# Seven-quarter W2 products, running sums added by an accumulating DMA, and a fixed weave in an attention and mixture-of-experts kernel

## The chip, the cores and the metric

The kernel runs on one core of a Trainium2 chip. The metric is device microseconds of one execution; lower is better. The kernel before took 844.76 us (median of 4 runs, 843.47 to 848.35); one profiled execution of it, from which the readings below come, had a span of 838.8 us (840.54 us as it was timed, a little less than any of the four). The names in profiles: PE is TensorE (PEld its weight loads), ACT is ScalarE, DVE is VectorE, POOL is GpSimd, SP is SyncE. An engine's name with a q is its DMA issuing or its sequencer.

## The reference, cut to what matters

```python
N, D, E, F = (3072, 512, 8, 1024)          # tokens, model width, experts, hidden width

def reference(q, k, v, proj, w_gate, w1, w2):
    x = masked_attention(q, k, v, proj)    # 4 batches of 768 tokens, 8 heads; [cut]
    P = exp(x @ w_gate - max)              # then 8 rounds of row and column scaling; [cut]
    out = zeros((N, D))
    for e in range(E):
        h = maximum(x @ w1[e], 0.0)        # "W1 product"
        ye = h @ w2[e]                     # "W2 product"
        out += P[:, e:e + 1] * ye
    return out
```

Every expert works on every token, so the second half of the program is 8 experts x 4 batches of 768 tokens. The change touches experts 1 to 7: 28 batches, which I name by expert and by b = 0 to 3. Expert 0 runs in the shadow of attention and routing.

## The kernel before: the parts that matter

The W1 product (`hidden`) already uses a Strassen-Winograd scheme: it is cut into 2 x 2 quarters and made of seven quarter products instead of eight, at the price of a few additions. GpSimd makes the sums of the weights (`quarters_of_w`), VectorE those of x. The W2 product (`combine`) is plain, and VectorE adds its result, times the routing weight, to the running sums `acc`. The W2 product of one batch is woven into the W1 product of the next, so that each engine's waits are covered by the other product. In the code, `pin(...)` keeps an instruction at its place in the program's order, and PSUM is the memory that matmuls write to.

```python
def load_w(e, which, pin=False):                     # 1 MB, cast to fp16 by GpSimd's DMA
    ...
    ins = nc.gpsimd.dma_start(out=t, in_=src)

def quarters_of_w(e):                                # called at b == 2 of the expert before
    if (e, 1) not in weights:
        load_w(e, 1, pin=True)
    ...
    s = spool.tile([P, 3, 2, F // 2], F16, tag="s1")
    pin(nc.gpsimd.tensor_tensor(s[:, 0], a21, a22, op=Alu.add))
    pin(nc.gpsimd.tensor_tensor(a21, a11, a21, op=Alu.subtract))
    pin(nc.gpsimd.tensor_tensor(s[:, 1], s[:, 0], a11, op=Alu.subtract))
    pin(nc.gpsimd.tensor_tensor(s[:, 2], a12, s[:, 1], op=Alu.subtract))

def combine(e, b):                                   # plain W2 product
    for j in range(J):                               # 6 blocks of 128 tokens
        yp = ... # a PSUM bank, 128 x 512
        for fo in range(FO):                         # 8 matmuls of 512 columns
            yield nc.tensor.matmul(yp, hT[:, fo, j * P:(j + 1) * P], w2[:, fo, :], ...)
            if fo == FO - 1:
                nc.vector.scalar_tensor_tensor(out=acc[:, blk, :], in0=yp, scalar=pw_[-1][:, blk, e:e + 1],
                                               in1=acc[:, blk, :], op0=Alu.mult, op1=Alu.add)
                if e == E - 1:
                    nc.sync.dma_start(out=outv[b, j], in_=acc[:, blk, :])
    # [cut: expert 0, the scaling in expert 1, the yields]

def woven(n):                                        # one step of each product in turn
    h = hidden(*work[n]) ...
    c = combine(*work[n - 1]) ...
    while more:
        more = run(h, True);  yield 650
        more = run(c, True) or more;  yield 650
```

The view of the output is `outv = out.rearrange("(b r j m) d -> b j m r d", ...)`: one block's output has the shape 4 x 32 x 512, which will matter.

The softmax here doesn't subtract the row's maximum and nothing guards it: scores larger than these inputs give would overflow.

## Time and profile before

| | before |
|---|---|
| median time | 844.76 us |
| span of the profiled run | 838.8 us |
| busy share of TensorE, VectorE, ScalarE, GpSimd | 94%, 52%, 47%, 20% |
| period of a batch (last ReLU copy of one batch to that of the next, on ScalarE) | 19.9 us in 25 of 27, 21.61 us in two of expert 1 |
| last matmul to the end of the span | 13.0 us |

These are lines of the page of the kernel before. The first line under part 1 is busy time and share of each engine. PEclk is TensorE's granted clock in tenths of full speed in 40 slices of the span. The line after it is the chain of waits that ended last, by engine. A group's line gives busy time, mean ns of one and idle time before it. The last line is a DMA issue with its size and the median us from issue to landing.

```profile
span 838.8 us, 13662 instructions
...
PE 786.6 (94%) x5404; PEld 427.1 (51%) x5404; DVE 440.2 (52%) x789; ACT 394.9 (47%) x698; POOL 165.8 (20%) x196
...
PEclk9879999999999999999999999999999999999997
...
PE 83%; DVE 6%; DMA 5%; ACT 2%; SPq 1%; issue 1%; POOL 1%; ACTq 0%; POOLq 0%; DVEq 0%
...
L155 PE MATMUL yp<-t,hT 128*128 128x512 f16 x1440 | 385.1, 379 | 0.0
...
L161 DVE SCALAR_TENSOR_TENSOR acc<-yp,p,acc 128x512 f32<-128x512 f32 x168 | 125.9, 749 | 114.0 <-PE yp L155 111.6
...
t<-in_moe_w_dram POOLq DMA_DIRECT2D x16, 1024.0 KB, 8.8
```

TensorE bounds the kernel: 83% of the chain are its matmuls. One batch period seen as a stretch says the same; the columns are the stretch, its length, busy us of PE, PEld, DVE, ACT and POOL with instruction counts, the clock, the DMA share and GB/s.

```profile
455.07:474.97 19.90, 19.76 (x106) 10.16 (x105) 10.73 (x19) 7.73 (x17) 0.00 (x0) 1.00 0.00 1
```

TensorE works 19.76 of 19.90 us at full clock, VectorE about half, GpSimd not at all. Once per expert GpSimd prepares the next W1. Its timeline (start, length, instruction, in brackets the idle time before it and what ended it) is:

```profile
417.05 0.75 POOL L120 DMA_DIRECT2D t<-in_moe_w_dram  x1 [58.10 <-PE d L520]
425.00 2.12 POOL L136 TENSOR_TENSOR s<-t 128x1024 f16<-128x1024 f16 x1 [7.20 <-DMA t<-in_moe_w_dram]
```

It issues the load, waits 7.20 us for it, and then runs four additions of 2.12 us. In this part of the program its queue holds nothing else but the load of W2.

### The profile page before, as it was taken

What the parts mean: (1) busy time and instruction counts of PE and PEld (TensorE: products, weight loads), DVE (VectorE), ACT (ScalarE), POOL (GpSimd) and SP (SyncE); (2) the same over time, 40 slices, a digit from 0 to 9 for tenths busy, and PEclk for the clock granted to TensorE, in tenths of its full rate; (3) what the DMA queues carried; (4) which work ended last, traced back from release to release, by engine and by line L of the source; (5) the groups of instructions that cost most, each with busy time, mean ns of one, the idle gap of its engine ahead of it and who ended that gap; (6) DMA issues with size and microseconds to landing.
All of it is one profiled execution on the core that took longest, in us unless ns stands there. A gap on an engine that the chain in (4) does not pass through costs nothing.

```text
span 838.8 us, 13662 instructions
## 1 busy us (share of the span) xinstructions
PE 786.6 (94%) x5404; PEld 427.1 (51%) x5404; DVE 440.2 (52%) x789; ACT 394.9 (47%) x698; POOL 165.8 (20%) x196
## 2 busy tenths in 40 slices
PE   3869999999889999999999999999999999999993
PEld 1546656666544544555555555555555555555551
DVE  3434646654476555555555555555555555555551
ACT  0857767678634555533333333333333333333330
POOL 7645245534031000400040004001300310000000
PEclk9879999999999999999999999999999999999997
DMA  6966677531020300230032023002300230001222
GB/s 176 263 155 155 136 182 192 130 73 27 1 51 2 51 0 1 51 51 1 3 51 48 1 47 47 9 1 51 50 1 1 51 51 1 1 0 52 77 81 92
DMA packets 31927, 50.60 MB, mean 60 GB/s; under 512 B 8504, under 2 KB 21304, under 8 KB 31864
## 3 DMA queue, kind: packets, MB, share of 16 engines
q0 software_dynamic: 16880, 33.30, 19.2%
q1 hardware_dynamic: 14316, 15.95, 7.0%
q8 instruction: 42, 0.69, 0.3%
q10 hardware_dynamic: 668, 0.49, 0.2%
q14 instruction: 21, 0.17, 0.1%
HBM read 53.14 MB, written 7.08 MB: 72 GB/s over the span
## 4 chain that ended last, share of the span: by engine, by line
PE 83%; DVE 6%; DMA 5%; ACT 2%; SPq 1%; issue 1%; POOL 1%; ACTq 0%; POOLq 0%; DVEq 0%
PE yp L155 34%; PE a L520 17%; PE d L520 14%; PE st L320 6%; PE hp L378 4%; DVE hT L529 4%; PE num L336 3%; PE yp L388 2%; ACT pt L323 2%; PE hp L177 1%; DMA ks<-t 1%; PE pr L243 1%; DMA v<-in_v_dram 1%; DMA acc<-in_q_dram 1%; DMA ds<-kb 1%
## 5 line engine op out<-in xcount | busy, mean ns | idle before, releaser
L155 PE MATMUL yp<-t,hT 128*128 128x512 f16 x1440 | 385.1, 379 | 0.0
L525 ACT COPY u<-a 128x384 f32<-128x384 f32 x336 | 161.1, 480 | 252.8 <-PE a L520 243.7
L529 DVE CUSTOM_DVE_ANT_0 hT<-d,u 128x384 f16<-128x384 f32 x336 | 179.3, 554 | 146.5 <-PE d L520 87.6
L155 PEld LDWEIGHTS <-hT 128*128 128x128 f16 x1440 | 140.9, 98 | 121.8 <-issue 0.8
L161 DVE SCALAR_TENSOR_TENSOR acc<-yp,p,acc 128x512 f32<-128x512 f32 x168 | 125.9, 749 | 114.0 <-PE yp L155 111.6
L323 ACT ACTIVATE pt<-st 128x768 f16<-128x768 f32 x192 | 147.2, 809 | 71.7 <-PE st L320 71.0
L520 PEld LDWEIGHTS <-t 128*128 128x128 f16 x896 | 87.8, 98 | 78.7 <-issue 10.8
L320 PE MATMUL st<-qs,ks 71*128 71x384 f16 x384 | 97.4, 336 | 18.4 <-DMA ks<-t 7.5
L520 PE MATMUL d<-xd,t 128*128 128x384 f16 x448 | 109.5, 326 | 3.9
L520 PEld LDWEIGHTS <-s 128*128 128x128 f16 x672 | 65.6, 98 | 87.0 <-issue 8.3
L520 PE MATMUL a<-xT,s 128*128 128x384 f16 x448 | 109.3, 326 | 0.0
L555 ACT ACTIVATE hT<-a 128x384 f16<-128x384 f32 x112 | 55.0, 491 | 73.9 <-PE a L520 73.4
L120 POOL DMA_DIRECT2D t<-in_moe_w_dram x16 | 13.5, 846 | 374.0 <-PE d L520 295.2
L336 PEld LDWEIGHTS <-pt 128*128 128x128 f16 x1152 | 62.3, 99 | 28.0 <-issue 3.0
L336 PE MATMUL num<-va,pt 128*128 128x65 f16 x1152 | 68.2, 196 | 0.6 <-ACT pt L323 0.6
L520 PE MATMUL a<-xd,s 128*128 128x384 f16 x224 | 55.1, 328 | 3.1 <-DVE xd L502 3.1
L520 PE MATMUL d<-xT,t 128*128 128x384 f16 x224 | 55.1, 328 | 0.0
L520 PE MATMUL a<-xT,t 128*128 128x384 f16 x224 | 55.0, 327 | 0.0
L320 PEld LDWEIGHTS <-ks 71*128 71x128 f16 x384 | 33.4, 100 | 39.3 <-issue 13.0
L232 POOL CAST t<-acc 128x768 f16<-128x768 f32 x32 | 26.3, 825 | 89.1 <-DVE acc L231 75.1
L381 DVE TENSOR_SCALAR hT<-hp 128x384 f16<-128x384 f32 x48 | 26.7, 555 | 28.6 <-PE hp L378 28.6
L378 PE MATMUL hp<-xT,t 128*128 128x384 f16 x192 | 39.0, 325 | 0.0
(74 smaller groups left out, 416.1 us busy)
## 6 DMA issues: line engine op xcount, KB each, us to landing
t<-in_moe_w_dram POOLq DMA_DIRECT2D x16, 1024.0 KB, 8.8
out_dram<-acc SPq DMA_DIRECT2D x24, 256.0 KB
acc<-in_k_dram POOLq DMA_DIRECT2D x7, 768.0 KB, 5.8
acc<-in_q_dram POOLq DMA_DIRECT2D x7, 768.0 KB, 5.9
v<-in_v_dram POOLq DMA_DIRECT2D x28, 192.0 KB, 4.6
ks<-t SPq DMA_DIRECT2D x64, 48.0 KB
qs<-t SPq DMA_DIRECT2D x56, 48.0 KB
acc<-in_k_dram SPq DMA_DIRECT2D x1, 768.0 KB
```

Of the source, the lines that this page charges most:

```text
L155: yield nc.tensor.matmul(yp, hT[:, fo, j * P:(j + 1) * P], w2[:, fo, :], start=(fo == 0), stop=(fo == FO - 1))
L161: nc.vector.scalar_tensor_tensor(out=acc[:, blk, :], in0=yp, scalar=pw_[-1][:, blk, e:e + 1], in1=acc[:, blk, :], op0=Alu.mult, op1=Alu.add)
L232: pin(nc.gpsimd.tensor_copy(t16s[name][:, c, :], trs[name][:, c, :]))
L320: pin(nc.tensor.matmul(st[:, i, 0:HT], d["k"][0:KR, h, kt * P:(kt + 1) * P], d["q"][0:KR, h, i * HT:(i + 1) * HT], start=True, stop=True))
L323: pin(nc.scalar.activation(out=pt, in_=st[:, :, 0:HT], func=Act.Exp, scale=scale))
L336: pin(nc.tensor.matmul(num[:, j * (D + 1):(j + 1) * (D + 1)], pf[:, j * P:(j + 1) * P], va[:, h, kt, :], start=(kt == 0 and j == 0), stop= ...
L378: pin(nc.tensor.matmul(hp[:, 0:HT], w1[:, do, fo * P:(fo + 1) * P], xT[:, do, b * S + t * HT:b * S + (t + 1) * HT], start=(do == 0), stop= ...
L381: pin(nc.vector.tensor_scalar(hT[:, fo, t * HT:(t + 1) * HT], hp[:, 0:HT], 0.0, None, op0=Alu.max))
L520: yield nc.tensor.matmul(bk, wq[wn][:, do, f * P:(f + 1) * P], xq[xn][:, do, :], start=first and do == 0, stop=do == 1, skip_group_check=True)
L525: nc.scalar.copy(t, bk)
L529: add(TENSOR_ADD_SAT, out=dst, in0=bk, in1=u, s0=3e38, s1=0.0)
L555: nc.scalar.activation(out=hT[:, f, hi], in_=a, func=Act.Relu)
```

## The change

The intent is to take TensorE's time down, since TensorE bounds the kernel. The W2 product is cut into quarters too: 3 pairs of token blocks x 7 products x 4 matmuls of 256 columns = 84 matmuls in place of 48 of 512. The additions this needs go where there was room. GpSimd makes the sums of W2 (`quarters_of_w2`, at b = 3), VectorE those of h (`sums_of_h`). Four of the seven results of a pair are read from one running PSUM bank by ScalarE, scaled, into a buffer `vt`, and one accumulating DMA in GpSimd's queue adds `vt` to `acc`. VectorE gathers the other three. The weave becomes a fixed string of steps: H is a step of the W1 product (`hidden`), C one of the W2 product (`mixed`).

```diff
+    def quarters_of_w2(e):                             # called at b == 3 of the expert before
         if (e, 2) not in weights:
+            load_w(e, 2, pin=True)
+        ...
+        pin(nc.gpsimd.tensor_tensor(t[:, 1], b22, b12, op=Alu.subtract))
+        pin(nc.gpsimd.tensor_tensor(b12, b12, b11, op=Alu.subtract))
+        pin(nc.gpsimd.tensor_tensor(t[:, 0], b22, b12, op=Alu.subtract))
+        pin(nc.gpsimd.tensor_tensor(t[:, 2], b21, t[:, 0], op=Alu.subtract))
+    def sums_of_h(e, b, i):                            # four VectorE operations, both operands in SBUF
+        pin(nc.vector.tensor_tensor(s_[:, 0], h21, h22, op=Alu.add))
+        pin(nc.vector.tensor_tensor(s_[:, 1], s_[:, 0], h11, op=Alu.subtract))
+        pin(nc.vector.tensor_tensor(h21, h11, h21, op=Alu.subtract))
+        pin(nc.vector.tensor_tensor(s_[:, 2], h12, s_[:, 1], op=Alu.subtract))
+    def mixed(e, b):
+        for i in range(J // 2):
+            vt = vkeep.tile([P, 4, DD // 2], F32, tag="v", name="vt")
+            ...                                        # 7 products; keep() for four, gather() for three
+            def keep(k, p):
+                pin(nc.scalar.activation(out=vt[:, k], in_=a, func=Act.Copy, scale=p))
+            def gather(k, src, p):
+                pin(nc.vector.scalar_tensor_tensor(out=dst, in0=src, scalar=p, in1=dst, ...))
+            for g, name in enumerate(ORDERS[i]):
+                step(name)
+                if g == 6:
+                    pin(nc.gpsimd.dma_start(out=acc[:, b, i], in_=vt, accum_op=Alu.add))
+                    if e == E - 1:                     # [cut: the last sum of all is done without it]
+                        pin((nc.gpsimd if final else nc.sync).dma_start(out=outv[b, j], in_=sums_of(b, j)...))
+    hspool = ctx.enter_context(tc.tile_pool(name="hspool", bufs=3))
+    vkeep = ctx.enter_context(tc.tile_pool(name="vkeep", bufs=3))
     def hidden(e, b):
         if b == 2 and e < E - 1:
             quarters_of_w(e + 1)
+        if b == 3 and e < E - 1:
+            quarters_of_w2(e + 1)
     def woven(n):
-        more = True
-        while more:
-            more = run(h, True); yield 650
-            more = run(c, True) or more; yield 650
+            plan = "HHCHCHCHCCH" + 3 * "HHCHCHCHCHCH" + "CH"
```

The cuts are the layout of `acc`, the pools that moved to make room, the sums of x, which are issued one at a time, and the pinned order of the W1 product and of expert 0.

## The prediction

> **What bounds it now.** In the view by stretches PE is busy 59.6 of each 60 us at clock 1.00; VectorE 32, ScalarE 23, GpSimd at most 10. The chain of waits from 380 us to the end is 92% matmuls (yp 48.7%, a 24.0%, d 19.4%). The timeline shows a 19.89 us period for each expert and batch (27 such periods): 56 matmuls of 384 columns at 162.5 ns (9.1 us), 48 of 512 at 216.7 ns (10.4 us), and two gaps of about 0.3 us.
>
> **What the change moves.** W2 products become 3 x 7 x 4 = 84 matmuls of 256 columns. The cost is linear (216.7/512 = 162.5/384), so 108.3 ns each: 9.1 us instead of 10.4. Weight loads keep up: attention's 65-column matmuls are 32 ns apart. A period is then 18.2 us, say 18.55 with gaps: 27 x 1.34 = 36 us off the critical path.
>
> Off the path, per period (estimated from like operations):
> - VectorE loses 6 x 749 ns, gains 12 fp16 additions of 512 (the 768-wide ones take 553 ns, so 0.42 us: 5.0 us) and 9 gathers of 256 (0.48 us: 4.3 us): 10.7 -> 16.0 us. 86% busy, in bursts of four additions (1.7 us).
> - ScalarE gains 12 scaled copies of 256 (about 0.38 us): 7.7 -> 12.3 us; expert 1's paired 0.72 us scalings cost about 3 us in all.
> - GpSimd gains three 512 KB accumulating DMAs per period and four more 2.12 us tensor operations per expert.
>
> **What gives some back.** GpSimd's order is load, four additions, then that period's accumulating DMAs, 12 times in all (W1 and W2 of six experts). Load and additions hold its queue 0.85 + 7.1 + 8.6 = 16.5 us, so the first sum's DMA leaves about 18 us into the period and lands 4 to 5 us later (768 KB loads land in 5.8). Its buffer (three, for three sums per period) is wanted again about 19.3 us in, and TensorE can run about a microsecond more: a 0 to 4 us stall. Second, VectorE's additions have two SBUF operands. The Trainium skill, "SBUF — State Buffer", section "Who interferes with whom", says these contend, as an exclusive lock, with a GpSimd instruction that reads SBUF. The trace agrees for another operation: the 192-wide kb scaling takes 0.39 to 0.77 us, ending when the GpSimd operation beside it ends. No run yet shows it for two-operand additions. If it holds in full, four additions behind four 2.1 us operations take 8 us, and y's single bank then stalls TensorE up to 5 us. Worst case 12 x 5 = 60 us; I take 1.4 us a time, 17 us.
>
> **Sum.** 844 - 36 + 3 + 17 = 828; leaning lower for gaps the fixed pattern removes: **826 us**, 80% range 806 to 868. Faster by over 2%: 0.52; within 2%: 0.28; slower: 0.20.
>
> **What would show it.** Right: period about 18.5 us for batches without weight preparation; 256-column matmuls 108 ns apart; in the two periods per expert with preparation, waits of ScalarE's vt copy on a DMA, and VectorE's hs additions lengthened from 0.42 towards 2 us beside GpSimd. Wrong: matmul spacing over 108 ns; waits spread over all periods (bursts on VectorE); vt waiting on DMAs everywhere (accumulating DMAs slower than 6 us each).
>
> **What would make it wrong.** Full lock on every addition (860 or more); or accumulating DMAs landing in 2 us and no lock (805 to 812).

## The result, and the profile after

The changed kernel is correct and took 913.62 us (median of 4 runs, 912.43 to 917.83) beside 844.76 us. The ratio of the fast runs is 1.0811, with a 95% interval of 1.0766 to 1.0856: 8% slower. The profiled execution is the one of 917.83 us, the slowest of the four.

These are the page's lines of the changed kernel that answer to those shown of before.

```profile
span 916.0 us, 16844 instructions
...
PE 781.9 (85%) x6412; PEld 536.5 (59%) x6412; DVE 560.0 (61%) x1213; ACT 516.7 (56%) x1033; POOL 300.0 (33%) x311
...
PEclk9879999999999899989998999889998998999965
...
PE 52%; DMA 23%; POOL 7%; issue 6%; ACT 5%; DVE 4%; SPq 1%; POOLq 0%; ACTq 0%; DVEq 0%
...
L201 PE MATMUL a<-t,hs 128*128 128x256 f16 x1008 | 162.3, 287 | 63.5 <-ACT vt L208 62.4
...
acc<-vt POOLq DMA_DIRECT2D x83, 512.0 KB, 5.1
t<-in_moe_w_dram POOLq DMA_DIRECT2D x16, 1024.0 KB, 11.2
```

TensorE's share of the chain fell from 83% to 52%; DMA rose from 5% to 23%. TensorE waited 62.4 us for `vt`, nearly all of it in eleven long gaps; and the weights' loads land later, 11.2 us instead of 8.8.

The stretches show both faces of the change: the first is a quiet batch, the second one that is stalled.

```profile
527.00:545.70 18.70, 18.70 (x145) 13.88 (x143) 14.12 (x33) 12.24 (x30) 2.51 (x4) 1.00 0.45 85
481.00:506.00 25.00, 19.20 (x128) 13.32 (x127) 14.62 (x31) 11.38 (x26) 11.67 (x8) 0.86 0.63 106
```

In the stalled stretch the clock is 0.86 and TensorE idles for 5.8 us. The period of every batch, measured as before:

| expert | b = 0 | b = 1 | b = 2 | b = 3 |
|---|---|---|---|---|
| 1 | (first) | 20.47 | 19.89 | 26.43 |
| 2 | 24.77 | 18.47 | 18.47 | 27.05 |
| 3 | 24.28 | 18.75 | 18.47 | 27.18 |
| 4 | 24.28 | 18.47 | 18.47 | 27.23 |
| 5 | 27.01 | 18.47 | 18.47 | 25.76 |
| 6 | 26.35 | 18.47 | 18.47 | 33.16 |
| 7 | 18.47 | 18.47 | 18.47 | 18.47 |

A quiet batch is 18.47 us, 1.42 less than the 19.89 of before, as intended. But b = 3 follows the preparation of W1 and costs 7.3 to 14.7 us more than quiet, and the next expert's b = 0, which follows that of W2, costs 5.8 to 8.5 us more. (For expert 6 both stalls fall into b = 3, and the next batch has none.) Together these excesses over 18.47 are 90 us, in twelve stalls.

How one such stall comes about stands in three timelines. GpSimd's queue first:

```profile
469.06 0.85 POOL L246 DMA_DIRECT2D acc<-vt  x1 [4.60 <-ACT hT L664]
469.60 1.09 POOL L113 DMA_DIRECT2D t<-in_moe_w_dram  x1
480.78 2.12 POOL L134 TENSOR_TENSOR s<-t 128x1024 f16<-128x1024 f16 x1 [10.09 <-DMA t<-in_moe_w_dram]
...
487.26 2.12 POOL L137 TENSOR_TENSOR s<-t,s 128x1024 f16<-128x1024 f16 x1
489.32 2.58 POOL L246 DMA_DIRECT2D acc<-vt  x3
490.98 1.85 POOL L113 DMA_DIRECT2D t<-in_moe_w_dram  x1
506.02 2.38 POOL L147 TENSOR_TENSOR t<-t 128x1024 f16<-128x1024 f16 x1 [13.20 <-DMA t<-in_moe_w_dram]
```

The queue works in order. The load of W1 is issued at 469.6, GpSimd stands 10.09 us waiting for it, adds for 8.6 us, and only at 489.32 come the accumulating DMAs of the whole batch, three at once. Then the load of W2 begins the same again, with 13.20 us of waiting. ScalarE and TensorE in the same stretch:

```profile
494.28 0.47 ACT L208 ACTIVATE vt<-a,p 128x256 f32<-128x256 f32 x1 [6.58 <-DMA acc<-vt]
```

```profile
488.51 0.49 PE L625 MATMUL d<-xd,t 128*128 128x384 f16 x2
494.80 1.01 PE L201 MATMUL a<-t,hs 128*128 128x256 f16 x4 [5.80 <-ACT vt L208]
...
497.10 1.06 PE L201 MATMUL a<-t,hs 128*128 128x256 f16 x4
...
499.79 0.60 PE L201 MATMUL a<-t,hs 128*128 128x256 f16 x4
```

All three `vt` buffers were full. ScalarE waited 6.58 us for the first accumulating DMA to land, and TensorE 5.80 us for ScalarE. After the gap four such matmuls soon take 1.06 us instead of 0.60: the clock is at half. The Trainium skill, "TensorE: Matmul & The Clock Gate", Part 1, says that the clock drops to half when TensorE has been idle for an activity window of about 3.4 us. The trace of the changed kernel agrees: between 300 and 862 us there are twelve gaps of 4.03 to 6.4 us (62 us in all), and half clock for 64.9 us, in pieces of 3.41 or 6.83 us at those gaps; between 255 and 829 us the kernel before has no half-clock piece. But less can be enough: in run 1 below, a single gap of 2.19 us (before 658.18 us) was followed by 3.41 us at half clock, and none of the gaps at its six half-clock pieces before the end is longer than 2.99 us. The excesses sum to 90 us and the gaps to 62, so about 28 us, or some 2.3 us a stall, are what the half clock costs (an estimate from these sums; TensorE worked for 51.3 of the 64.9 us at half clock, and by that count it lost about 26 us).

Eleven of the twelve gaps end with ScalarE's `vt` copy, as this one does. The twelfth, at 778.86 us, does not. There GpSimd's additions happen to meet VectorE's sums of h:

```profile
774.74 2.12 POOL L147 TENSOR_TENSOR t<-t 128x1024 f16<-128x1024 f16 x1 [13.32 <-DMA t<-in_moe_w_dram]
774.76 2.38 DVE L177 TENSOR_TENSOR hs<-hs,hT 128x512 f16<-128x512 f16 x1
...
782.96 1.00 PE L201 MATMUL y<-t,hT 128*128 128x256 f16 x4 [4.10 <-DVE acc L215]
```

A sum of h that takes 0.42 us elsewhere takes 2.38 us, the next two the same, VectorE's gathers come late, and TensorE waits 4.10 us for one of them.

At the end more time is lost. The issues of the outputs on SyncE (start, time from first to last, count), first of before, then of after:

```profile
799.78 27.46 SPq L164 DMA_DIRECT2D out_dram<-acc  x12
```

```profile
849.89 48.70 SPq L249 DMA_DIRECT2D out_dram<-acc  x9
898.69 8.68 SPq L254 DMA_DIRECT2D out_dram<-acc  x3
```

and two pieces of the chain of waits at the end of after (start, length, what):

```profile
868.40 9.47 DMA acc<-vt
...
879.58 17.26 DMA acc<-vt
```

The last matmul ends at 879.6 and the span at 916.0: 36.4 us, where before had 13.0. Accumulating DMAs that land in 5.1 us elsewhere take 9.47 and 17.26 us here, and single output issues take up to 11.34 us (at most 0.63 before).

The whole account of the span, from the two traces:

| term | us |
|---|---|
| first batch ends earlier (269.1 instead of 273.5) | -4.4 |
| 27 periods at 18.47 instead of 19.89 | -38 |
| twelve stalls, beyond 18.47 | +90 |
| last W2 product, which has nothing woven into it (11.6 to 17.8 us) | +6 |
| last matmul to the end (13.0 to 36.4 us) | +23.4 |
| sum (measured: 916.0 - 838.8) | +77 |

The medians lie only 69 us apart. The other 8 us come from the choice of executions: the profiled one of before was faster than its four timed runs, and that of after was the slowest of its own. Some 3.7 us that the other periods, most of them expert 1's, take beyond 18.47 or 19.89 us stand in both kernels and are left out.

### The profile page after: what moved, and what is told of

Its sections match the earlier page's. It is cut to its first block, busy times and chain, and to the rows that moved or that the text cites. A ratio compares the mean times of both kernels' runs of the same rounds, so it can differ in the third digit from the quotient of the medians.

```text
span 916.0 us, 16844 instructions
## 1 busy us (share of the span) xinstructions
PE 781.9 (85%) x6412; PEld 536.5 (59%) x6412; DVE 560.0 (61%) x1213; ACT 516.7 (56%) x1033; POOL 300.0 (33%) x311
## 4 chain that ended last, share of the span: by engine, by line
PE 52%; DMA 23%; POOL 7%; issue 6%; ACT 5%; DVE 4%; SPq 1%; POOLq 0%; ACTq 0%; DVEq 0%
PE a L201 10%; PE a L625 10%; DMA t<-in_moe_w_dram 9%; DMA acc<-vt 8%; PE d L625 7%; PE y L201 5%; PE st L418 5%; PE hp L476 3%; PE num L434 2%; PE yp L159 2%; ACT pt L421 2%; PE yp L486 2%; PE d L201 2%; POOL t L135 1%; POOL s L136 1%
## 5 line engine op out<-in xcount | busy, mean ns | idle before, releaser
L208 ACT ACTIVATE vt<-a,p 128x256 f32<-128x256 f32 x335 | 158.5, 473 | 233.5 <-PE a L201 167.0
L634 DVE CUSTOM_DVE_ANT_0 hT<-d,u 128x384 f16<-128x384 f32 x336 | 185.1, 553 | 168.9 <-ACT u L630 163.8
L201 PE MATMUL a<-t,hs 128*128 128x256 f16 x1008 | 162.3, 287 | 63.5 <-ACT vt L208 62.4
L246 POOL DMA_DIRECT2D acc<-vt x83 | 71.0, 972 | 333.6 <-ACT vt L208 119.9
L201 PEld LDWEIGHTS <-hT 128*128 128x128 f16 x1344 | 134.1, 100 | 61.1 <-issue 9.6
L201 PEld LDWEIGHTS <-hs 128*128 128x128 f16 x1008 | 102.7, 102 | 107.5 <-issue 58.0
L625 PE MATMUL a<-xT,s 128*128 128x384 f16 x448 | 116.4, 343 | 0.1
L201 PE MATMUL y<-t,hT 128*128 128x256 f16 x672 | 106.6, 284 | 5.1 <-DVE acc L215 5.0
L215 DVE SCALAR_TENSOR_TENSOR acc<-y,p,acc 128x256 f32<-128x256 f32 x168 | 80.3, 478 | 17.2 <-PE y L201 17.1
L625 PEld LDWEIGHTS <-s 128*128 128x128 f16 x672 | 67.8, 101 | 19.4 <-issue 2.3
L418 PEld LDWEIGHTS <-ks 71*128 71x128 f16 x384 | 33.4, 100 | 38.5 <-issue 13.1
## 6 DMA issues: line engine op xcount, KB each, us to landing
t<-in_moe_w_dram POOLq DMA_DIRECT2D x16, 1024.0 KB, 11.2
```

Source lines behind the costliest of these rows:

```text
L201: pin(nc.tensor.matmul(dst, hq[hn][:, fo, :], wq[wn][:, fo, :], start=first and fo == 0, stop=fo == FH - 1, skip_group_check=True))
L208: pin(nc.scalar.activation(out=vt[:, k], in_=a, func=Act.Copy, scale=p))
L215: pin(nc.vector.scalar_tensor_tensor(out=dst, in0=src, scalar=p, in1=dst, op0=Alu.mult, op1=Alu.add))
L246: pin(nc.gpsimd.dma_start(out=acc[:, b, i], in_=vt, accum_op=Alu.add))
L418: pin(nc.tensor.matmul(st[:, i, 0:HT], d["k"][0:KR, h, kt * P:(kt + 1) * P], d["q"][0:KR, h, i * HT:(i + 1) * HT], start=True, stop=True))
L625: pin(nc.tensor.matmul(bk, wq[wn][:, do, f * P:(f + 1) * P], xq[xn][:, do, :], start=first and do == 0, stop=do == 1, skip_group_check=True))
```

## The experiments

Three theories were to be told apart; the expectations name them by letters. A fourth, **D**, stands in the first two expectations: that accumulating DMAs are too slow in general, wherever they stand.

- **Q**, the queue: the accumulating DMAs stand in GpSimd's queue behind a load that has not landed and four additions. Their buffers stay full, ScalarE waits, TensorE waits, and the clock halves.
- **L**, the lock, its rival: GpSimd's additions shut VectorE out, so the sums of h come late. The Trainium skill, "SBUF — State Buffer", section "Who interferes with whom", says that a VectorE instruction with two SBUF inputs contends with a GpSimd instruction that reads SBUF, and that the pair of ports is an exclusive lock.
- **T**, the tail: the end is long because an output of shape 4 x 32 x 512 runs on few DMA engines. The Trainium skill, "DMA: Bandwidth & Descriptors", section "Why a DMA increments its semaphore by 16 and not by 1", says that the number of engines is the largest one up to 16 that divides the slowest dimension of both sides. With a slowest dimension of 4 that would be 4 engines. No view of the profile names the engines of a DMA, so this number is an estimate from the page's rule. Runs 3 and 11 test the time, and what the traces show of the packets is told with run 11.

All eleven kernels computed the right result. The kernel before, run beside them, had medians of 845.07 us (runs 1 to 4), 843.25 us (5 to 8) and 844.32 us (9 to 11).

### 1. A fourth vt buffer

```diff
-    hspool = ctx.enter_context(tc.tile_pool(name="hspool", bufs=3))
-    vkeep = ctx.enter_context(tc.tile_pool(name="vkeep", bufs=3))
+    hspool = ctx.enter_context(tc.tile_pool(name="hspool", bufs=2))
+    vkeep = ctx.enter_context(tc.tile_pool(name="vkeep", bufs=4))
```

> The changed kernel with a fourth buffer for the kept sums (and two instead of three for the sums of h, to make room). Theory Q (GpSimd's queue, held by the weight load and its four additions, delays the accumulating DMA, and ScalarE waits for the buffer): the buffer is wanted one third of a batch (about 6 us) later, so the 12 stalls shrink by about 6 us each: stalls after W1 preparation 8.7 -> about 3 us, after W2 6 -> about 0; time 913 -> 845 to 860. Theory L (port lock between VectorE's and GpSimd's additions): unchanged, 905 to 920. Theory D (accumulating DMAs too slow for the DMA engines in general): a buffer only delays the stall, 895 or more.

Measured: 872.26 us, ratio 1.0351 (1.0284 to 1.0417): between the ranges of Q, L and D, so none foresaw the time. The batches after a W1 preparation fell to 19.3 to 20.0 us, so the fourth buffer takes nearly the whole W1 stall away. Those after a W2 preparation stayed at 24.3 to 25.3 us, but with another cause, as these lines of the waits say (engine, what it waited for, us in total, times, longest):

```profile
PE a L201 <- DVE hs L177: 19.0, 12, 3.0
...
ACT vt L208 <- DMA acc<-vt: 7.7, 5, 2.1
```

In the changed kernel the second of these waits is:

```profile
ACT vt L208 <- DMA acc<-vt: 66.5, 12, 7.2
```

So ScalarE's wait for the accumulating DMA fell to 7.7 us in all, and now TensorE waits for the sums of h. The smaller `hspool` is not the cause of that: batches without a preparation still take 18.47 us, and after each W2 preparation three of the sums of h last 2.2 to 2.3 us, beside additions of GpSimd. Q is supported, and there is something behind it: taking the first wait away let a second show.

### 2. Loads one batch earlier

```diff
     def hidden(e, b):
+        if b == 1 and e < E - 1:
+            load_w(e + 1, 1, pin=True)
         if b == 2 and e < E - 1:
             quarters_of_w(e + 1)
+            load_w(e + 1, 2, pin=True)
```

The weights have then landed when the additions' turn comes, so GpSimd's queue is held only while it adds (9.2 us from the first addition below to the end of the fourth), not some 20 us.

> The changed kernel with each weight load issued one batch before its additions, so GpSimd's queue no longer stands still for a load to land. Theory Q: the hold falls from about 20 us to about 10 us, ScalarE's waits for the accumulating DMA (66 us in 12 waits) go to under 5 us, every batch takes 18.5 us: 913 -> 822 to 832. Theory L: the additions now begin at the start of a batch and meet the hs additions of VectorE there; stalls of 3 to 8 us in each of the 12 batches with additions remain or appear: 860 to 920. Theory D: ScalarE's waits on the DMA stay above 40 us, 880 or more.

Measured: 899.1 us, ratio 1.0648 (1.0592 to 1.0703). The wait for the DMA is gone:

```profile
ACT vt L208 <- DMA acc<-vt: 1.9, 2, 1.1
```

That rules out D, which forecast over 40 us. And yet b = 2 and b = 3 of experts 1 to 6, where the additions now run, take 24.31 us, three of the first four of them 24.8 to 25.2: 5.85 us or more too much, twelve times. All others take 18.47 but two of expert 1's sums (20.47 and 19.51) and one of 18.75. The timeline of VectorE and GpSimd shows why:

```profile
403.13 0.42 DVE L176 TENSOR_TENSOR hs<-hT 128x512 f16<-128x512 f16 x1
403.28 0.84 POOL L246 DMA_DIRECT2D acc<-vt  x1 [4.60 <-ACT hT L667]
403.58 2.98 DVE L177 TENSOR_TENSOR hs<-hs,hT 128x512 f16<-128x512 f16 x1
403.84 2.42 POOL L147 TENSOR_TENSOR t<-t 128x1024 f16<-128x1024 f16 x1
...
406.35 2.19 POOL L148 TENSOR_TENSOR t<-t 128x1024 f16<-128x1024 f16 x1
406.48 2.34 DVE L178 TENSOR_TENSOR hT<-hT 128x512 f16<-128x512 f16 x1
...
408.62 2.18 POOL L149 TENSOR_TENSOR t<-t 128x1024 f16<-128x1024 f16 x1
408.74 2.33 DVE L179 TENSOR_TENSOR hs<-hT,hs 128x512 f16<-128x512 f16 x1
...
410.87 2.19 POOL L150 TENSOR_TENSOR t<-t 128x1024 f16<-128x1024 f16 x1
```

An addition of VectorE that takes 0.42 us alone takes 2.3 to 3.0 us, and ends 0.3 us after GpSimd's ends; the two engines take turns. Three additions wait for one of GpSimd's each. The skill's lock is thus seen for two-operand additions, and in full. And the waits say that TensorE pays:

```profile
PE a L201 <- DVE hs L177: 22.4, 12, 1.9
...
PE y L201 <- DVE hT L178: 15.9, 12, 1.3
```

What follows: Q and L are both true, and in the changed kernel Q hid L. There the additions of GpSimd waited for their load, and in eleven of the twelve preparations they met only one of the sums of h (1.4 to 2.4 us long in the trace), with no gap of over 1 us on TensorE that ends with it; in the twelfth they met three.

### 3. Outputs in four parts

```diff
-                            pin((nc.gpsimd if final else nc.sync).dma_start(
-                                out=outv[b, j], in_=sums_of(b, j).rearrange("p c d -> p (c d)")))
+                            for m in range(M4):
+                                pin((nc.gpsimd if final else nc.sync).dma_start(
+                                    out=outv[b, j][m],
+                                    in_=sums_of(b, j)[R * m:R * (m + 1)].rearrange("p c d -> p (c d)")))
```

The same for the halves of the last sum. Each part has 32 rows as its slowest dimension.

> The changed kernel with each 256 KB output written by four DMAs of 32 partitions instead of one whose target's slowest dimension is 4. Theory T (the long end, 36 us from the last matmul to the end of the span against 13 before, comes from outputs that use four DMA engines, which the accumulating DMAs use too): the end shrinks to 12 to 18 us, the output issues on the SP queue no longer take up to 11 us, 913 -> 888 to 897, and nothing else changes. Rival (the end is the chain accumulate, wait, output, on GpSimd's queue in order): 907 to 914.

Measured: 892.27 us, ratio 1.0574 (1.0527 to 1.062). The 27 periods together are as in the changed kernel (593.5 and 592.7 us), and the end, from the last matmul, takes 15.6 us instead of 36.4. In its chain the accumulating DMAs that took 9.47 and 17.26 us are:

```profile
869.90 5.40 DMA acc<-vt
...
879.55 5.14 DMA acc<-vt
```

T's forecast holds in the time (888 to 897), in the end (12 to 18 us) and in the issues, and the rival, the order of GpSimd's queue alone (907 to 914), is out. Four times as many issues of a quarter the size end 21 us sooner, and the accumulating DMAs beside them no longer suffer.

### 4. Both: early loads and outputs in four parts

The edit is that of 2 and 3 together.

> Both of the last two. Theories Q and T together: 913 - 85 - 20 = 803 to 815, that is faster than the kernel before by 3.5 to 5%. If the stalls only hide one another (the rivals): 850 or more.

Measured: 874.37 us, ratio 1.0349 (1.0295 to 1.0402): a miss, since this was written before the result of 2 was known and counted on Q alone. The batches with additions take 24.3 us (25.26 and 24.79 in expert 1), as in 2; the end takes 15.9 us, as in 3. The two effects add: 14.5 and 21.4 us alone, 39.3 together (in 2 the end was 42.6 us, longer than in the changed kernel, so that 3's edit had more to win).

### 5. Additions spread out, behind the issues of the accumulating DMAs

This is 4 with the eight additions of an expert taken apart. `quarters_of_w` and `quarters_of_w2` become generators, and one or two additions are issued after a sum's accumulating DMA.

```diff
+            # additions of the next expert's weights behind this sum: 8 in the batches 0 to 2
+            count = {(0, 1): 2, (1, 0): 1, (1, 1): 2, (2, 0): 1, (2, 1): 2}.get((b, i), 0) if e < E - 1 else 0
             for g, name in enumerate(ORDERS[i]):
                 ...
                         pin(nc.gpsimd.dma_start(out=acc[:, b, i], in_=vt, accum_op=Alu.add))
+                    for _ in range(count):
+                        next(preps[e + 1])
```

> Early loads and four-part outputs as in e4, and the eight weight additions of an expert issued one or two at a time right behind an accumulating DMA, where VectorE has no hs addition for the next 2 to 6 us, instead of four in a row at the start of a batch. Theory L (what e2 and e4 still lose, 5.85 us in each of 12 batches, is VectorE's two-operand hs additions shut out by GpSimd's additions): those batches fall from 24.3 to 18.5 us, the hs additions to a mean of 0.42 to 0.50 us, 874 -> 800 to 812. Rival (GpSimd's queue is still the cause, through late accumulating DMAs): the additions still stand in that queue, so 840 or more.

Measured: 809.33 us, ratio 0.9599 (0.9562 to 0.9637): 4.0% faster than before. Every batch takes 18.47 or 18.48 us but the four in which expert 1's sums are scaled (19.52 to 22.08 us) and one of 18.75. The sums of h take 0.42 to 0.44 us in the mean, where 2 had 0.45 to 0.79. The Winograd scheme's gain was there all the time; the placement of GpSimd's work, and the shape of the outputs (run 10), decided whether it was seen.

### 6. The same additions, on VectorE

```diff
-            preps[e + 1] = chain(quarters_of_w(e + 1, nc.gpsimd), quarters_of_w2(e + 1, nc.gpsimd))
+            preps[e + 1] = chain(quarters_of_w(e + 1, nc.vector), quarters_of_w2(e + 1, nc.vector))
```

> As e5, but the eight additions run on VectorE, at the same places. Theory L: without a GpSimd operation that reads SBUF no hs addition is lengthened; VectorE gets 8 x about 0.7 us more per expert, at most 2 us of it lost per expert: 802 to 820. Rival (VectorE, at 15 us of 18.5, is itself the limit): each expert loses the 5.6 us, 835 or more.

Measured: 808.42 us, ratio 0.9582 (0.9553 to 0.9611), the same as 5. Now no addition of GpSimd is left here that could hold up VectorE, and batches take 18.47 to 19.14 us after expert 1, no less than in 5. So nothing of L was left in 5 outside expert 1.

### 7. No accumulating DMA: VectorE gathers all seven

```diff
             def keep(k, p):
-                if last and k == 1:
-                    gather(k, a, p)
-                    return
+                gather(k, a, p)
+                return
...
-                    if not last:
-                        pin(nc.gpsimd.dma_start(out=acc[:, b, i], in_=vt, accum_op=Alu.add))
```

It starts from 5.

> As e5, but the kept sums are added by VectorE straight from PSUM: no scaled copy on ScalarE, no accumulating DMA. VectorE then has 6.6 + 5.0 + 21 x 0.478 = 21.7 us of work per batch. If VectorE's work bounds it, batches take 21.7 to 24 us and the time is 890 to 950; if the accumulating DMA cost more than it saves, it is below e5.

Measured: 982.42 us, ratio 1.1647 (1.1608 to 1.1687). Quiet batches take 22.51 us, in the expected range: VectorE, with twelve gathers more, now bounds them. The total is above the expectation, because b = 1 takes 33.4 to 34.8 us (37.6 in expert 1). Without the accumulating DMAs between them, GpSimd's additions bunch: of the eight for expert 4, six run from 478.7 to 495.7 us, the last four in a row, and the sums of h beside them take up to 2.33 us. But the quiet batches alone are 4 us longer than in 5, so the accumulating DMA is worth having. What hurt was its place in the queue.

This run also answers how the accumulating DMAs act on the loads. Without them GpSimd's wait for W1 is as it was in the kernel before (7.20 us there, 10.09 in the changed kernel), as a line of GpSimd's timeline in this run shows:

```profile
464.41 2.11 POOL L135 TENSOR_TENSOR s<-t 128x1024 f16<-128x1024 f16 x1 [7.27 <-DMA t<-in_moe_w_dram]
```

The twelve loads for experts 2 to 7 land 7.9 to 10.1 us after their issue here, 7.7 to 8.9 in the kernel before, and 10.5 to 16.0 in the changed kernel.

### 8. The fixed weave alone

The W2 product stays plain and VectorE gathers as in before, but everything is pinned and woven by the fixed string of H and C.

```diff
+        if n < len(work):
             plan = "".join("HC" if i % 7 else "H" for i in range(28))
-        elif n < len(work):
-            plan = "HHCHCHCHCCH" + 3 * "HHCHCHCHCHCH" + "CH"
         else:
-            plan = 21 * "C"
+            plan = 24 * "C"
```

`mixed` is then the plain `combine` with its order pinned.

> The changed kernel with W2 products plain (48 matmuls of 512 columns, one VectorE update per block, no accumulating DMA): of the change only the fixed pattern of both products is left. Theory: the pattern removes the two gaps of 0.3 us per batch, 19.89 -> 19.55 us: 845 -> 832 to 840. Rival: it has no effect of its own, 841 to 847.

Measured: 837.21 us, ratio 0.9933 (0.9898 to 0.9967). That is within the range of the theory (832 to 840), but by luck: the batches still take 19.89 us and not 19.55, so the expected gain from the weave is a miss; the two gaps of 0.3 us of before have another cause, which I did not look for. Some 2 us of the small gain are in expert 1, whose batches take 20.2 to 20.35 us (up to 21.6 before); where the rest is was not found.

### 9. The best version that these runs point to

From 5: expert 2's additions, which are made during expert 1, go to VectorE (in 5 GpSimd's met the sums of x there); VectorE adds all sums of the last batch, so no accumulating DMA stands between the last matmul and the outputs; and the last outputs are spread over three queues.

```diff
-            preps[e + 1] = chain(quarters_of_w(e + 1, nc.gpsimd), quarters_of_w2(e + 1, nc.gpsimd))
+            eng = nc.vector if e == 1 else nc.gpsimd
+            preps[e + 1] = chain(quarters_of_w(e + 1, eng), quarters_of_w2(e + 1, eng))
...
-                if last:
+                if final:
                     dst = acc[:, b, i, k, :]
                     pin(nc.vector.tensor_tensor(dst, dst, vt[:, k], op=Alu.add))
...
-                    if not last:
+                    if not final:
                         pin(nc.gpsimd.dma_start(out=acc[:, b, i], in_=vt, accum_op=Alu.add))
```

> e5 with three mends: expert 2's weights are prepared on VectorE (in e5 those two batches took 21.2 and 22.1 us), in the last batch every kept sum is added by VectorE and no accumulating DMA is left at the end, and the last outputs are divided over three queues. From the parts: 5 us and about 8 us less than e5: 794 to 800. If the end is set by the outputs and not by the accumulating DMAs: 802 to 806.

Measured: 800.74 us (797.7 to 803.55), ratio 0.9483 (0.9436 to 0.953): 5.2% faster than before. The median is 0.7 us above the expected range. The end takes 9.6 us, and the four batches of expert 1's sums at most 20.48 us. The page's lines:

```profile
PE 753.3 (95%) x6412; PEld 525.0 (66%) x6412; DVE 540.8 (68%) x1229; ACT 515.2 (65%) x1033; POOL 285.1 (36%) x309
...
PEclk9779999999999999999999999999999999999998
```

TensorE is busy 95% again, with no dip of the clock in the expert stage.

### 10. Number 5 with outputs as in the changed kernel

The edit of 3 taken back from 5.

> e5 without the four-part outputs (early loads and spread additions only). Theory T (the outputs' few DMA engines, shared with the accumulating DMAs, make the long end): 20 to 25 us above e5, 828 to 836. If e5's shorter end came from the spread additions: within 5 us of e5.

Measured: 835.23 us, ratio 0.9899 (0.9849 to 0.9949). The end takes 38.2 us instead of 15.7. The tail is worth over 20 us whatever the batches do.

### 11. The kernel before with outputs in four parts

```diff
-                        nc.sync.dma_start(out=outv[b, j], in_=acc[:, blk, :])
+                        for m in range(M4):
+                            nc.sync.dma_start(out=outv[b, j][m], in_=acc[R * m:R * (m + 1), blk, :])
```

> The kernel before with its outputs in four parts: no accumulating DMAs there. Theory T: six outputs leave in the last 10 us, one per 1.73 us, and wait for one another; that costs it 4 to 8 us of its 13 us end: 836 to 840. If few DMA engines hurt only beside accumulating DMAs: 842 to 847.

Measured: 835.25 us, ratio 0.989 (0.9848 to 0.9931), just below T's range. The end takes 5.7 us instead of 13.0. So the shape costs time even with no accumulating DMA beside it.

The trace files also keep single packets, which no view of the profile lists. In the kernel before, the 24 outputs of 256 KB have 3072 packets of 2 KB and 96 of 4 bytes that close them, four to an output; the last two outputs finish 2.57 us apart, though a new one is issued every 1.73 us, so they queue up. In this run there are 1536 closing packets, 16 to each part; the packets of the last output run up to 16 at a time and take 1.86 us. In the same way ScalarE's one output at the end of the changed kernel has at most 4 packets under way at once and takes 6.7 us, and its four parts in run 3 have up to 9 and take 2.3 us. Four and 16 are the numbers of the skill's rule.

Part of the gain of 5 and 9 is thus to be had without the change. Against this kernel, 5 is 3.1% faster and 9 is 4.1% faster (medians, and for 5 from another call of runs).

## Why the prediction was wrong

- **"27 x 1.34 = 36 us off the critical path": right.** The quiet batch is 18.47 us, where 18.55 was predicted, and 27 x 1.42 = 38 us came off. Runs 5, 6 and 9 show the gain nearly whole.
- **The places of the cost: right.** The stalls stand in the two batches per expert that follow a preparation, ScalarE's `vt` copy waits for a DMA, and the accumulating DMA lands in 5.1 us (4 to 5 predicted).
- **"Worst case 12 x 5 = 60 us; I take 1.4 us a time, 17 us": this is the step that failed.** The twelve stalls measured 90 us, 7.5 us each. Two things were missing. The sum took a landing of 7.1 us after the issue, from a trace with no accumulating DMAs; beside them GpSimd waited 10.09 and 13.20 us for its loads, as shown above, and without them, in run 7, it waited 7.27 us. That holds the queue 3 to 6 us longer, and the stall that had been put at 0 to 4 us became a gap of 4.0 to 6.4 us. Second, such a gap is long enough to halve the clock, and costs some 2.3 us more at half speed; the prediction priced a wait at its own length.
- **The end: not in the prediction at all.** It cost 23.4 us, and the last W2 product with nothing woven into it 6 us more. The prediction spoke of batches only. Runs 3 and 10 give the end's cause: 21 to 22 us of it go away with the shape of the outputs (and 3 us of the last W2 product's, which takes 14.4 us in run 3 instead of 17.8).
- **The lock: right in mechanism, and one stall of twelve.** In the changed kernel the sums of h took 0.44 to 0.58 us in the mean; each preparation made one of them 1.4 to 2.4 us long, but three in a row only in expert 6 (the gap of 4.10 us). When the loads came early (2), three met every time, and it cost 5.85 us in each of twelve batches. "Up to 5 us" was the right size for a case that the changed kernel mostly did not have.

Against all this, the range of 806 to 868 us was too low even at its upper end: its "full lock on every addition (860 or more)" was the worst that I had thought of, and the queue behind a slower load was not in it at more than 4 us.

What stays open: that the accumulating DMAs slow the loads is shown by run 7, but what they contend for is not known. Nor is it known what makes the batches of expert 1's sums 1 us or more longer in nearly every version (the prediction's 3 us for them is about what the changed kernel's first two show, 2.0 + 1.4 us, but the kernel before loses as much, so that it is no difference); runs 6 and 9 only show that moving GpSimd's additions takes part of it away.

## What to carry to other kernels

When work moves into an idle engine's queue, list what stands ahead of it in that queue and what that waits for: an addition that waits for a load blocks every later DMA of the queue, and the time a load takes to land has to be taken under the traffic that the change itself adds. Put the load far ahead, and the additions singly behind the DMAs that must not wait, away from VectorE's two-operand work; and remember that a wait of TensorE can cost more than its length: here gaps of 4.0 to 6.4 us cost about half as much again through the clock (28 us on 62, by the estimate above). Cost the beginning and the end of a change apart from its periods, and look at the slowest dimension of the outputs' shape.

## What the Trainium skill lacked or had wrong

- "DMA: Bandwidth & Descriptors" has no rate for an accumulating DMA from SBUF to SBUF. Here 512 KB landed in 5.1 us (median of 83 issues), and up to 17.26 us beside outputs of shape 4 x 32 x 512; 1 MB loads beside such DMAs landed in 10.5 to 16.0 us, against 7.7 to 8.9 in the kernel before.
- The same page gives the rule for the number of engines by the slowest dimension, but no cost. Here outputs of shape 4 x 32 x 512, against four of 32 rows each, made the end 36.4 us instead of 15.6, and in the kernel before 13.0 instead of 5.7. The traces show four closing packets to a DMA of the first kind and 16 to one of the second; that this number, and not the smaller size of the DMAs, makes the difference is argued, not shown.
- No page that I read warns that an accumulating DMA waits in GpSimd's queue behind an instruction that waits for a load: here the queue stood closed to them for some 20 us (469.6 to 489.3 us), and eleven of the twelve stalls come from that (the twelve cost 90 us together).
- "SBUF — State Buffer" has the lock right for two-operand additions. The size seen here: 0.42 us alone, 2.3 to 3.0 us behind a GpSimd addition of 2.2 us, and a batch 5.85 us longer where GpSimd's four additions held up three sums of h (run 2).
- "TensorE: Matmul & The Clock Gate" puts the drop of the clock after an idle window of about 3.4 us. In the changed kernel that agrees with the trace (gaps of 4.03 to 6.4 us, half clock in pieces of 3.41 or 6.83 us), but in run 1 a single gap of 2.19 us was followed by 3.41 us at half clock, so there less than a whole idle window was enough.
